# Decoding's intermediate word in PSUM, low-half products in a row, and other slots for the second batch's keys and values and the last weight's halves

## The chip, the cores and the metric

The kernel runs on one core of a Trainium2 chip, as one launch. The metric is device microseconds of that core, lower is better. The core has five engines that run their own instructions in order and wait for each other through semaphores: TensorE (PE, matmuls out of SBUF into PSUM; its weight loads are PEld), VectorE (DVE), ScalarE (ACT), GpSimd (POOL), and SyncE (SP), which issues all the DMA transfers here. SBUF and PSUM have 128 partitions; PSUM has eight banks of 512 float32 per partition, all in use.

## The reference

Three stages; q, k and v are float32, the weights float64:

```python
scores = scale * q @ k.T                      # 4 batches, 8 heads, 576 x 576, head size 64
kth = 32nd largest of each row
attn = softmax(where(scores >= kth, scores, -1e9))
x = (attn @ v) as [2304, 512]
h = x @ w_in;  x = (h * sigmoid(h)) @ w_out   # 512 -> 2048 -> 512
h = x @ w2_in; x = elu(h) @ w2_out            # 512 -> 2048 -> 512
```

The four weight matrices have 512 x 2048 elements each and arrive as float64, 8.4 MB a matrix.

## The kernel before

**Slots.** The work is a hand-ordered software pipeline, `slot(s)` for s from about -5 to 176. The 2304 rows are 18 chunks of 128, and each chunk has 8 heads, which makes 144 attention tiles: slot s holds tile s. In its slot and the next a tile gets its 32nd largest score by four MAX8 (L561) with three replacements between them (L565), and a mask with the row sum (L589), all on VectorE; ScalarE takes the exponential (L576) and the half-precision copy (L615), POOL the remainder of that copy (L621, L622), SyncE transposes both (L624), and TensorE multiplies by the values (L643) three slots later. The product of queries and keys for tile s+1 (L529) goes to TensorE in slot s, into one of two score tiles. VectorE's list of each slot is interleaved by `dv`: one operation of the top-32, then up to `per` steps of decoding.

The two MLPs follow in steps of a quarter chunk, the first from slot 13 on (`LAG`), the second from slot 25: TensorE makes h (L699), ScalarE and POOL make the activation (L727 and a subtraction L164), and two slots later TensorE multiplies by the second weight into bank `a` (L747).

**Decoding.** A weight is 16 pieces of 128 x 512 float64. A transfer (L249) brings a piece's words into a staging place (parts of W that are empty yet, for the last weight also tiles of the MLP). ScalarE or POOL shifts the low word (L259, L261). VectorE takes the high word: L271 masks and shifts it, L274 merges in the sign and exponent bit, in the same place f of W; POOL adds the low word (L277), which gives float32. The pieces lie in slots -2 to 12 by the table `PIECES` (3, 3, 4, six times 5, six times 4), 16 a weight; ten pieces of the last weight come as two halves (256 wide). Loads of the third weight stand in the slots in which the same places have just been decoded, some in the slot that decodes them.

**Scale and low halves.** When a weight is decoded, TensorE sums its Gram matrix (`w_gram`, 64 matmuls, L291, bank `a`), VectorE takes the trace a slot later (`w_trace`, L296), TensorE adds it over the partitions (L173), and a power-of-two scale follows. For the first three weights ScalarE then writes the high half (L308), TensorE forms the scaled remainder in PSUM (`w_lo`, L314 and L315) and ScalarE copies it out as the low half (L319). This goes by pairs of pieces at three points of a slot (`w_point`), in the three slots behind each weight's end, 3, 3 and 2 pairs. The last weight is scaled on ScalarE and split on POOL instead (`w_split`, L333 and L164), one or two pieces a slot.

**Second batch's keys and values.** They are loaded, squared and summed, scaled, split and stored to DRAM ahead of use (`k_keep`, `v_keep`), a key pair every four slots from slot 17 on and a value pair two slots behind each; they come back by transposing (L405) or plain loads when the chunk begins that needs them, from slot 31 on.

PSUM holds two score tiles of two banks, two rotating banks `h` (both for the MLP's h and for the low halves), one bank `a` and one for the attention output.

Of the kernel before, what the change touches and what calls it, by code (L numbers as in the profile page):

```python
# [32 lines left out]
def kernel(  # L33
# [52 lines left out]
    dram = pool("dram", 1, space=bass.MemoryType.DRAM)  # L86
    p2_p = pool("p2", 6)
    ps_s = pool("ps_s", 2, space=PSUM)
    ps_h = pool("ps_h", 2, space=PSUM)
    ps_a = pool("ps_a", 1, space=PSUM)  # L90
    ps_v = pool("ps_v", 1, space=PSUM)

# [170 lines left out]
    def w_dec_ops(j, n, e=None):  # L263
        f = w_raw(j, n, Wi)
        if e is not None:
            f = f[:, e * 256:(e + 1) * 256]
        def word(x):
            return raws[j, n, e].rearrange("p (x two) -> p x two", two=2)[:, :, x]

        def first():  # L270
            nc.vector.tensor_scalar(f, word(1), 0x07FFFFFF, 3, op0=ALU.bitwise_and, op1=ALU.logical_shift_left)  # L271

        def second():
            nc.vector.scalar_tensor_tensor(  # L274
                f, word(1), -(1 << 30), f, op0=ALU.bitwise_and, op1=ALU.bitwise_or
            )
            nc.gpsimd.tensor_tensor(f, f, word(0), op=ALU.add)  # L277

        return [first, second]
# [30 lines left out]
    los = {}  # L310

    def w_lo(j, n):
        ps = ps_h.tile([128, 512], F32, tag="h", name="lo")
        nc.tensor.matmul(out=ps, lhsT=eye[:, 128 * j:128 * j + 128], rhs=w_raw(j, n), start=True, stop=False)  # L314
        nc.tensor.matmul(out=ps, lhsT=minus, rhs=W[:, j * NWP + n, 0:DM], start=False, stop=True)  # L315
        los[j, n] = ps
# [368 lines left out]
    def emit_in(l, ch, i):  # L685
        if (l, i) == (0, 0):

            t = small.tile([128, 1], F32, tag="c1", name="c1")
            nc.gpsimd.tensor_scalar(t, ixs[:, xc(ch):xc(ch) + 1], sW[0][1], 0.5, op0=ALU.mult, op1=ALU.mult)
            c1[ch] = t  # L690
        xt = xts[l, ch]
        ps = ps_h.tile([128, 512], F32, tag="h", name="h")
        for u in range(4):
            for kk in range(KDM):
                n = 2 * l * NWP + i * 4 + kk
                f = u * 128
                wh, wl = W[:, n, f:f + 128], W[:, n, 512 + f:512 + f + 128]
                for x, (w, z) in enumerate(((wh, kk), (wh, KDM + kk), (wl, kk))):
                    nc.tensor.matmul(  # L699
                        out=ps[:, f:f + 128],  # L700
                        lhsT=w,
                        rhs=xt[:, z, :],
                        start=(kk == 0 and x == 0),
                        stop=(kk == KDM - 1 and x == 2),
                    )
        hps[l, ch, i] = ps
# [100 lines left out]
    LDB = 28  # L807
    LAG = 13
    LAG2 = 12
    SPLIT = (3, 3, 3)  # L810
    PIECES = (3, 3, 4, 5, 5, 5, 5, 5, 5, 4, 4, 4, 4, 4, 4)
    ON_ACT = 3

# [25 lines left out]
    for (b, i), t in first_use.items():  # L839
        x = dict(b=b, i=i)  # L840
        if b == 0:
            prep((t - 5, t - 4, t - 3), partial(k_load, **x), partial(k_sum, **x), True,
                 partial(k_ops, **x), partial(k_hi, **x), partial(k_lo, **x))
            late[t - 2].append((partial(k_tp, **x), None))
            prep((t - 1, t, t + 1), partial(v_load, **x), partial(v_sum, **x), True,
                 partial(v_ops, **x), partial(v_hi, **x), partial(v_lo, **x))
        else:
            d = 2 if b == 1 else 4
            r = first[b] - 35 + 2 * d * i + (19 if b == 1 else 2 * (b % 2))
            prep((r - 1, r + 1, r + 2), partial(k_load, **x), partial(k_sum, **x), True,  # L850
                 partial(k_ops, **x), partial(k_hi, **x), partial(k_keep, **x))
            late[t - 3].append((partial(k_tp, **x), None))
            r += d
            prep((r - 1, r + 1, r + 2), partial(v_load, **x), partial(v_sum, **x), True,
                 partial(v_ops, **x), partial(v_hi, **x, keep=True), partial(v_keep, **x))
            loads[t].append(partial(v_back, **x))
# [10 lines left out]

    wload, wnow = defaultdict(list), defaultdict(list)

    points, grams, traces, hi_late = {}, defaultdict(list), defaultdict(list), defaultdict(list)  # L870

    def spread(s, counts):
        return {(n, None): s + x for n, x in enumerate(x for x, c in enumerate(counts) for _ in range(c))}
# [5 lines left out]
    for j, d in dec.items():  # L879
        end = max(d.values()) + 1  # L880
        for x, s in d.items():
            decs[s].append((j, *x))
        grams[end - 1].append(j)
        traces[end].append(j)
        if j == 3:
            for (n, _), x in spread(end, (1, 1, 1, 1, 1, 1, 1, 2, 2, 1, 1, 1, 1, 1)).items():
                late[x].append((partial(w_scaled, j, n), None))
                splits[x + 1].append(partial(w_split, j, n))
            continue
        hi_late[end].append((j, 0))  # L890
        for p in range(NWP // 2):
            points[end + 1 + p // SPLIT[j], p % SPLIT[j]] = (j, p)
    late[15].append((w_const, lambda: None))
    for n in range(NWP):
        wload[(-5, -5, -4, -4, -4, -4, -3, -3, -2, -2, -2, -1, -1, -1, -1, -1)[n]].append((0, n, None))
# [8 lines left out]
    def w_point(s, p):  # L904
        if (s, p) not in points:
            return lambda: None
        j, x = points[s, p]
        for n in (2 * x, 2 * x + 1):
            w_lo(j, n)

        def rest():
            for n in (2 * x, 2 * x + 1):
                w_put(j, n)
            if 2 * x + 2 < NWP:
                w_hi2(j, x + 1)

        return rest

# [185 lines left out]
```

## Time and profile before

| what | value |
|---|---|
| median of three runs | 1182.84 us (1180.58 to 1187.54) |
| the profiled execution | 1180.23 us, its span 1178.5 us |
| busy share of the span | PE 86%, DVE 84%, ACT 74%, POOL 71% |
| mean granted TensorE clock | 0.967 |
| L277, POOL's addition | 75 in all, 55 of them at 1418 ns on average |
| L621, L727, L164 (gh) on POOL | 1162, 1271, 1160 ns on average |

A row of the 40 slices has a digit for each fortieth of the span, the busy share in tenths. In a table of stretches each row has the stretch, its length, and then for each engine the busy time and the number of instructions that start in it; at the end stand the granted clock, the share of the DMA engines and GB/s. A row of one line has the count, then the shortest, middle and longest duration in ns. A row of the timeline has start, duration, engine, line, operation and tiles, and in brackets how long the engine had been idle and what ended that.

### The profile page before, as it was taken

How to read it: one execution, taken by the hardware profiler on the slowest of the kernel's cores; microseconds unless marked ns; L12 is line 12 of the kernel's file. 1: busy time of each engine (PE TensorE's matmuls, PEld its weight loads, DVE VectorE, ACT ScalarE, POOL GpSimd, SP SyncE). 2: the span in 40 equal slices, each digit the busy share in tenths (PEclk: the TensorE clock that was granted, in tenths of full speed). 3: DMA queues.
4: the chain of work that ended last, by engine and by line, in shares of the span. 5: the costliest groups of instructions: out<-in, count | busy, mean ns of one | idle time of the engine just before them, and what ended most of it. 6: DMA issues, size and time to landing. Idle time of an engine off the chain costs nothing.

```text
span 1178.5 us, 30959 instructions
## 1 busy us (share of the span) xinstructions
PE 1016.3 (86%) x11974; PEld 727.3 (62%) x11974; DVE 984.5 (84%) x2215; ACT 875.6 (74%) x1568; POOL 841.4 (71%) x1026
## 2 busy tenths in 40 slices
PE   0057667858889999999999999999999999999997
PEld 0033233645657777677766777677777777777765
DVE  7999999997878899998988999898989999995000
ACT  6347767668787788888877888888777877777654
POOL 6777886779777667778776777677776776666643
PEclk9967889979999999999999999999999999999999
DMA  9867674353668746555567756556773654433100
GB/s 324 248 196 197 211 186 123 78 110 90 121 129 141 150 91 130 102 115 112 108 129 144 142 95 122 98 99 132 121 135 67 107 91 83 83 61 68 28 8 21
DMA packets 387157, 141.37 MB, mean 120 GB/s; under 512 B 362945, under 2 KB 370113, under 8 KB 387009
## 3 DMA queue, kind: packets, MB, share of 16 engines
q1 hardware_dynamic: 387008, 139.39, 55.7%
q8 instruction: 94, 1.54, 0.5%
q14 instruction: 55, 0.44, 0.1%
HBM read 52.17 MB, written 21.10 MB: 62 GB/s over the span
## 4 chain that ended last, share of the span: by engine, by line
PE 32%; POOL 19%; DVE 16%; DMA 15%; issue 10%; ACT 7%; SPq 1%; POOLq 0%; ACTq 0%; DVEq 0%
PE a L747 14%; PE h L699 14%; DMA et<-e 10%; POOL e L621 5%; DVE W L274 4%; POOL t L727 4%; DVE W L271 4%; DVE m L561 3%; POOL gh L164 3%; DVE r L565 3%; PE S L529 2%; PE av L643 2%; POOL e L622 1%; DMA vd<-v 1%; DMA W<-in_moe_w_in_dram 1%
## 5 line engine op out<-in xcount | busy, mean ns | idle before, releaser
L699 PE MATMUL h<-xt,W 128*128 128x128 f16 x6912 | 411.3, 220 | 2.0 <-DMA xt<-x 2.0
L747 PE MATMUL a<-W,gh 128*128 128x512 f16 x1728 | 401.6, 382 | 12.2 <-ACT o L793 5.8
L699 PEld LDWEIGHTS <-W 128*128 128x128 f16 x6912 | 396.3, 98 | 15.0 <-issue 4.5
L561 DVE MAX8 m<-r 128x8 f32<-128x576 f32 x432 | 312.9, 750 | 2.3
L747 PEld LDWEIGHTS <-gh 128*128 128x128 f16 x1728 | 160.3, 98 | 189.4 <-issue 11.6
L621 POOL TENSOR_TENSOR e<-e,e 128x512 f16<-128x512 f32 x144 | 167.4, 1162 | 139.2 <-ACT e L615 130.8
L164 POOL TENSOR_TENSOR gh<-t,gh 128x512 f16<-128x512 f32 x144 | 167.0, 1160 | 71.0 <-ACT gh L731 71.0
L565 DVE MATCH_REPLACE8 r<-m,r 128x576 f32<-128x576 f32 x288 | 214.0, 743 | 0.0
L727 POOL TENSOR_TENSOR t<-u,t 128x512 f32<-128x512 f32 x144 | 183.0, 1271 | 29.4 <-ACT u L721 23.1
L731 ACT ACTIVATE gh<-t 128x512 f16<-128x512 f32 x144 | 90.2, 627 | 116.0 <-POOL t L727 114.8
L529 PE MATMUL S<-kt,qt 128*128 128x288 f16 (+1 forms) x640 | 99.4, 297 | 64.0 <-DVE e L589 24.9
L576 ACT ACTIVATE e<-S,bias,c 128x576 f32<-128x576 f32 x144 | 119.8, 832 | 43.8 <-DVE r L565 36.3
L561 DVE MAX8 m<-S 128x8 f32<-128x576 f32 x144 | 109.6, 761 | 50.8 <-PE S L529 50.3
L615 ACT ACTIVATE e<-e 128x576 f16<-128x576 f32 x144 | 97.4, 677 | 59.7 <-DMA et<-e 26.9
L529 PEld LDWEIGHTS <-qt 128*128 128x128 f16 (+1 forms) x640 | 56.4, 102 | 134.5 <-issue 52.1
L589 DVE SCALAR_TENSOR_TENSOR e<-S,m,e 128x576 f32<-128x576 f32 x144 | 115.4, 802 | 0.1
L565 DVE MATCH_REPLACE8 r<-m,S 128x576 f32<-128x576 f32 x144 | 107.7, 748 | 0.0
L643 PE MATMUL av<-vt,et 128*128 128x64 f16 (+1 forms) x2240 | 91.6, 195 | 17.3 <-DMA et<-e 17.2
L643 PEld LDWEIGHTS <-et 128*128 128x128 f16 (+1 forms) x2240 | 80.1, 102 | 28.7 <-DMA et<-e 21.6
L314 PE MATMUL lo<-W,eye 128*128 128x512 f32 x96 | 63.7, 751 | 31.1 <-ACT W L319 22.8
L277 POOL TENSOR_TENSOR W<-W 128x512 int32<-128x512 int32 (+1 forms) x55 | 77.0, 1418 | 17.8 <-DVE W L274 7.9
L574 ACT ACTIVATE bias<-m,fixed,c 128x1 f32<-128x1 f32 x144 | 54.0, 375 | 11.1 <-DVE m L561 11.1
(125 smaller groups left out, 1218.5 us busy)
## 6 DMA issues: line engine op xcount, KB each, us to landing
W<-in_moe_w_in_dram SPq DMA_DIRECT2D x32, 512.0 KB, 6.9
W<-in_moe_w_out_dram SPq DMA_DIRECT2D x22, 512.0 KB, 5.9
qd<-q SPq DMA_DIRECT2D x34, 256.0 KB, 4.3
kn<-in_k_dram SPq DMA_DIRECT2D x16, 288.0 KB, 3.2
qn<-in_q_dram SPq DMA_DIRECT2D x16, 256.0 KB, 3.6
out_dram<-o SPq DMA_DIRECT2D x16, 256.0 KB, 2.8
vd<-v SPq DMA_DIRECT2D x12, 320.0 KB, 3.7
vt<-vd SPq DMA_DIRECT2D x24, 160.0 KB, 2.7
```

The lines of the kernel that those rows point to most:

```text
L164: nc.gpsimd.tensor_tensor(dst, x, hi, op=ALU.subtract)
L529: nc.tensor.matmul(out=ps[n * e:n * e + n, a, 0:HALF], lhsT=qt[:, 2 * (t % 2) + p, n * e:n * e + n], rhs=kt[:, a * HALF:(a + 1) * HALF], s ...
L561: nc.vector.max(st["m8"][:, i, :], src if i == 0 else st["r"])
L565: nc.vector.match_replace(out=fold(r) if i == 0 else r, in_to_replace=st["m8"][:, i, :], in_values=src if i == 0 else r, imm_value=LOW,)
L576: nc.scalar.activation(out=fold(e), in_=src, func=AF.Exp, scale=c[:, 0:1], bias=bias)
L589: nc.vector.scalar_tensor_tensor(e, src, st["m8"][:, n - 1, 7:8], e, op0=ALU.is_ge, op1=ALU.mult, accum_out=acc)
L615: nc.scalar.activation(out=h[:, 0:S], in_=e32s[t], func=AF.Copy)
L621: nc.gpsimd.tensor_tensor(h[:, S + LO:2 * S], e[:, 0:SF], h[:, 0:SF], op=ALU.subtract)
L643: nc.tensor.matmul(out=o, lhsT=et[:, c, n * e:n * e + n], rhs=r, start=(i == 0), stop=(i == len(seq) - 1))
L699: nc.tensor.matmul(out=ps[:, f:f + 128], lhsT=w, rhs=xt[:, z, :], start=(kk == 0 and x == 0), stop=(kk == KDM - 1 and x == 2),)
L727: nc.gpsimd.tensor_tensor(t, u, t, op=ALU.add if l else ALU.mult)
L747: nc.tensor.matmul(out=acc, lhsT=gh[:, z, u * 128:(u + 1) * 128], rhs=W[:, n, w * 512:(w + 1) * 512], start=(m == 0 and x == 0), stop=(m = ...
```

## The change

Five things, all in the work before slot 40:

1. L271 writes its word into a new PSUM tile y in bank `h0`, and L274 reads it from there and writes f as before. POOL's addition is unchanged. The two banks `h` no longer rotate but have names, `h0` and `h1`; the MLP alternates them by step.
2. The low-half products use `h1` for even pieces and bank `a` for odd ones, and `h1` for both in the slots in which the Gram sum holds `a` (slots 3, 6, 9, 14).
3. Their pairs form one list over the three weights, filled from slot 4 to 13 into the points that are free: three a slot, one in slots 6 and 9. Pairs end in slot 13 instead of 12.
4. The last weight's Gram sum and trace come one slot later, its scaling begins in slot 14 instead of 13, and the two doubled slots move: 17 and 19 for the scaling instead of 20 and 21.
5. The second batch's key pairs go by 16, 21, 27, 32 (before 18, 22, 26, 30) and its value pairs by 18, 24, 30, 35 (before 20, 24, 28, 32).

```diff
-    ps_h = pool("ps_h", 2, space=PSUM)
+    ps_h = pool("ps_h", 1, space=PSUM)
...
         def first():
-            nc.vector.tensor_scalar(f, word(1), 0x07FFFFFF, 3, op0=ALU.bitwise_and, op1=ALU.logical_shift_left)
+            y.append(ps_h.tile([128, 512], F32, tag="h0", name="y").bitcast(I32)[:, 0:f.shape[1]])
+            nc.vector.tensor_scalar(y[0], word(1), 0x07FFFFFF, 3, op0=ALU.bitwise_and, op1=ALU.logical_shift_left)
 
         def second():
             nc.vector.scalar_tensor_tensor(
-                f, word(1), -(1 << 30), f, op0=ALU.bitwise_and, op1=ALU.bitwise_or
+                f, word(1), -(1 << 30), y[0], op0=ALU.bitwise_and, op1=ALU.bitwise_or
             )
...
     def w_lo(j, n):
-        ps = ps_h.tile([128, 512], F32, tag="h", name="lo")
+        ps = ps_a.tile([128, 512], F32, tag="a", name="lo") if n % 2 and slot_now[0] not in held else ps_h.tile([128, 512], F32, tag="h1", name="lo")
...
-        ps = ps_h.tile([128, 512], F32, tag="h", name="h")
+        ps = ps_h.tile([128, 512], F32, tag=f"h{i % 2}", name="h")
...
-            d = 2 if b == 1 else 4
-            r = first[b] - 35 + 2 * d * i + (19 if b == 1 else 2 * (b % 2))
+            d, r = 4, first[b] - 35 + 8 * i + 2 * (b % 2)
+            if b == 1:
+                r, d = ((16, 2), (21, 3), (27, 3), (32, 3))[i]
...
-        grams[end - 1].append(j)
-        traces[end].append(j)
+        grams[end - (j < 3)].append(j)
+        traces[end + (j == 3)].append(j)
+        held.add(end + (j == 3))
         if j == 3:
-            for (n, _), x in spread(end, (1, 1, 1, 1, 1, 1, 1, 2, 2, 1, 1, 1, 1, 1)).items():
+            for (n, _), x in spread(end + 1, (1, 1, 1, 2, 1, 2, 1, 1, 1, 1, 1, 1, 0, 1, 1)).items():
...
+    pairs = [(j, p) for j in range(3) for p in range(NWP // 2)]
+    free = [(s, p) for s in range(ends[0] + 1, LAG + 1) for p in range(3) if p == 2 or s not in held]
+    points = dict(zip(free, zip(pairs, pairs[1:] + [None])))
```

VectorE in slot 1, where the first weight's last pieces are decoded between two tiles' top-32 operations (W is the weight array, S scores, r the row without the values found, m8 the maxima). Before:

```order
L561 MAX m8_336<-S_297 128x8
L271 TENSOR_SCALAR W_135<-W_135 128x512 [waits DMAHW6_49]
L274 SCALAR_TENSOR_TENSOR W_135<-W_135 128x512 [waits DVE_49]
L565 MATCH_REPLACE r_280<-m8_279,r_280 128x576
L271 TENSOR_SCALAR W_135<-W_135 128x512 [waits DMAHW7_49]
```

and in the changed kernel:

```order
L564 MAX m8_347<-S_307 128x8
L274 TENSOR_SCALAR y_350<-W_135 128x512 [waits DMAHW6_49,DVE_49]
L277 SCALAR_TENSOR_TENSOR W_135<-W_135,y_350 128x512 [waits DVE_49]
L568 MATCH_REPLACE r_287<-m8_286,r_287 128x576
L274 TENSOR_SCALAR y_355<-W_135 128x512 [waits DMAHW7_49,DVE_49]
```

Nothing moved; the first operation writes y, the second reads it, and the first also waits for VectorE's own operation before, since y has one buffer. All later line numbers are three or more higher.

TensorE at the end of slot 5, the last low-half product of the slot and the beginning of the second weight's Gram sum. Before:

```order
L315 MATMUL lo<-W,eye 128x512 [waits Activation_49]
L291 LDWEIGHTS W
L291 MATMUL gram<-W 128x128
```

and in the changed kernel:

```order
L318 MATMUL lo<-W,eye 128x512 [waits Activation_49]
L294 LDWEIGHTS W
L294 MATMUL gram<-W 128x128 [waits Activation_49]
```

The order is the same, but the Gram sum now waits for ScalarE, which copies the odd product out of the bank. The sums of the third and fourth weight have the same wait.

POOL in slot 22 (e16 is the exponentials' remainder, t and gh the MLP, x16 the second MLP's input, W a piece of the last weight). Before:

```order
L621 TENSOR_TENSOR e16_2588<-e32_2445,e16_2588 128x512
L622 TENSOR_TENSOR e16_2588<-e32_2445,e16_2588 128x64
L727 TENSOR_TENSOR t_2567<-u_2566,t_2567 128x512
L164 TENSOR_TENSOR x16_2599<-y_2371,x16_2599 128x512
L333 TENSOR_SCALAR W_135<-W_135 128x512
L164 TENSOR_TENSOR W_135<-W_135 128x512
L333 TENSOR_SCALAR W_135<-W_135 128x512
L164 TENSOR_TENSOR W_135<-W_135 128x512
L164 TENSOR_TENSOR gh_2677<-t_2567,gh_2677 128x512
```

and in the changed kernel:

```order
L624 TENSOR_TENSOR e16_2673<-e32_2541,e16_2673 128x512
L625 TENSOR_TENSOR e16_2673<-e32_2541,e16_2673 128x64
L730 TENSOR_TENSOR t_2652<-u_2651,t_2652 128x512
L164 TENSOR_TENSOR x16_2685<-y_2462,x16_2685 128x512
L336 TENSOR_SCALAR W_135<-W_135 128x512
L164 TENSOR_TENSOR W_135<-W_135 128x512
L164 TENSOR_TENSOR gh_2759<-t_2652,gh_2759 128x512
```

One of the two pieces that were split here has moved to another slot.

## Rows read from the trace of the kernel before

**Rows 1.** The page's 40 slices, busy tenths of VectorE

```profile
DVE  7999999997878899998988999898989999995000
```

**Rows 2.** Table of stretches, all engines: busy us (instructions), clock, DMA share, GB/s

```profile
44.10:106.30 62.20, 26.84 (x153) 13.83 (x154) 60.58 (x112) 34.83 (x65) 48.41 (x47) 0.79 0.71 203
106.30:146.60 40.30, 30.66 (x171) 15.66 (x170) 36.93 (x74) 31.19 (x57) 30.96 (x30) 0.84 0.71 210
146.60:204.40 57.80, 40.36 (x206) 19.04 (x204) 56.84 (x111) 38.79 (x72) 44.77 (x58) 0.87 0.64 159
...
265.40:319.90 54.50, 44.41 (x543) 32.43 (x544) 42.95 (x112) 45.50 (x83) 47.79 (x59) 0.97 0.45 100
...
400.80:1074.00 673.20, 654.66 (x8274) 488.39 (x8273) 620.10 (x1441) 542.13 (x968) 485.05 (x619) 1.00 0.58 108
```

**Rows 3.** Table of stretches, VectorE's L271 alone (first four), then L274 alone

```profile
0.00:44.10 44.10, 14.21 (x15) 1.00 0.95 305
44.10:106.30 62.20, 16.07 (x20) 0.79 0.71 203
106.30:146.60 40.30, 7.73 (x13) 0.84 0.71 210
146.60:204.40 57.80, 16.50 (x26) 0.87 0.64 159
...
0.00:44.10 44.10, 14.65 (x15) 1.00 0.95 305
44.10:106.30 62.20, 21.55 (x20) 0.79 0.71 203
106.30:146.60 40.30, 12.63 (x12) 0.84 0.71 210
146.60:204.40 57.80, 18.32 (x25) 0.87 0.64 159
```

**Rows 4.** Single lines L271 and L274: shortest, middle, longest ns

```profile
L271 DVE TENSOR_SCALAR W<-W x55: 401/824/2352, 6.8 to 199.9; 128x512 int32<-128x512 int32 x54, 128x256 int32<-128x256 int32 x1
...
L274 DVE SCALAR_TENSOR_TENSOR W<-W x55: 665/911/1771, 7.2 to 200.5; 128x512 int32<-128x512 int32 x54, 128x256 int32<-128x256 int32 x1
...
L274 DVE SCALAR_TENSOR_TENSOR W<-gh,W x6: 424/426/597, 155.0 to 198.9; 128x256 int32<-128x256 int32 x6
```

**Rows 5.** Timeline, two POOL additions and the VectorE operations issued during them

```profile
19.53 1.34 POOL L277 TENSOR_TENSOR W<-W 128x512 int32<-128x512 int32 x1 [0.68 <-DVE W L274]
19.77 1.65 DVE L274 SCALAR_TENSOR_TENSOR W<-W 128x512 int32<-128x512 int32 x1
...
35.60 1.28 POOL L277 TENSOR_TENSOR W<-W 128x512 int32<-128x512 int32 x1 [1.14 <-DMA vn<-in_v_dram]
36.12 1.05 DVE L271 TENSOR_SCALAR W<-W 128x512 int32<-128x512 int32 x1
```

**Rows 6.** Single lines of VectorE with one operand in PSUM

```profile
L760 DVE TENSOR_SCALAR y<-a x18: 671/673/692, 242.9 to 1131.9; 128x512 f32<-128x512 f32 x18
...
L589 DVE SCALAR_TENSOR_TENSOR e<-S,m,e x144: 793/801/819, 43.3 to 1073.7; 128x576 f32<-128x576 f32 x144
```

**Rows 7.** Timeline in slot 5: the loads' issue, and POOL waiting for one

```profile
96.11 2.65 SPq L249 DMA_DIRECT2D W<-in_moe_w_in_dram  x5
...
100.42 0.88 POOL L261 TENSOR_SCALAR W<-W 128x512 int32<-128x512 uint16 x1 [3.82 <-DMA W<-in_moe_w_in_dram]
```

**Rows 8.** Timeline of TensorE, the fourth weight's Gram sum at the end of slot 12

```profile
204.95 3.83 PE L291 MATMUL gram<-W 128*128 128x128 bf16 x64
```

**Rows 9.** Costs of splitting on POOL (205 to 330 us), and VectorE's gap (timeline)

```profile
L164 POOL TENSOR_TENSOR W<-W 128x512 f16<-128x512 f32 x16 | 18.5, 1159 | 1.3
...
L333 POOL TENSOR_SCALAR W<-W 128x512 f16<-128x512 f32 x16 | 9.9, 621 | 0.6 <-ACT W L161 0.6
...
278.52 0.16 DVE L133 TENSOR_SCALAR p<-S 128x1 int32<-128x1 int32 x1 [5.71 <-PE S L173]
```

**Rows 10.** Timeline, VectorE's wait for the first keys' sum

```profile
15.06 0.16 DVE L133 TENSOR_SCALAR p<-S 128x1 int32<-128x1 int32 x1 [1.15 <-PE S L173]
```

More of the change, by code (lines that the diff above doesn't have):

```diff
@@ L268, in word @@
             return raws[j, n, e].rearrange("p (x two) -> p x two", two=2)[:, :, x]
+        y = []
         def first():
-            nc.vector.tensor_scalar(f, word(1), 0x07FFFFFF, 3, op0=ALU.bitwise_and, op1=ALU.logical_shift_left)
+            y.append(ps_h.tile([128, 512], F32, tag="h0", name="y").bitcast(I32)[:, 0:f.shape[1]])
+            nc.vector.tensor_scalar(y[0], word(1), 0x07FFFFFF, 3, op0=ALU.bitwise_and, op1=ALU.logical_shift_left)
         def second():
             nc.vector.scalar_tensor_tensor(
-                f, word(1), -(1 << 30), f, op0=ALU.bitwise_and, op1=ALU.bitwise_or
+                f, word(1), -(1 << 30), y[0], op0=ALU.bitwise_and, op1=ALU.bitwise_or
             )
@@ L809 @@
     LAG2 = 12
-    SPLIT = (3, 3, 3)
     PIECES = (3, 3, 4, 5, 5, 5, 5, 5, 5, 4, 4, 4, 4, 4, 4)
@@ L868 @@
     wload, wnow = defaultdict(list), defaultdict(list)
-    points, grams, traces, hi_late = {}, defaultdict(list), defaultdict(list), defaultdict(list)
+    ends, held, grams, traces, hi_late = [], set(), defaultdict(list), defaultdict(list), defaultdict(list)
     def spread(s, counts):
@@ L889 @@
             continue
-        hi_late[end].append((j, 0))
-        for p in range(NWP // 2):
-            points[end + 1 + p // SPLIT[j], p % SPLIT[j]] = (j, p)
+        ends.append(end)
+    pairs = [(j, p) for j in range(3) for p in range(NWP // 2)]
+    free = [(s, p) for s in range(ends[0] + 1, LAG + 1) for p in range(3) if p == 2 or s not in held]
+    points = dict(zip(free, zip(pairs, pairs[1:] + [None])))
+    hi_late[ends[0]].append(pairs[0])
     late[15].append((w_const, lambda: None))
@@ L906, in w_point @@
             return lambda: None
-        j, x = points[s, p]
+        (j, x), more = points[s, p]
         for n in (2 * x, 2 * x + 1):
@@ L913, in rest @@
                 w_put(j, n)
-            if 2 * x + 2 < NWP:
-                w_hi2(j, x + 1)
+            if more:
+                w_hi2(*more)
         return rest
```

## The prediction

> **What bounds the kernel now.** I read the table of 40 slices first [rows 1]: VectorE is nearly full from the second slice to the thirty-sixth, that is through the whole attention, so averages don't tell which engine sets the pace where. So I cut the span at the ends of VectorE's mask operation (L589), one per slot, and read the busy times of these stretches [rows 2]. Between 44.1 and 106.3 us VectorE works 60.58 of 62.20 us, and between 146.6 and 204.4 us 56.84 of 57.80: there it sets the pace, with GpSimd (POOL) at 48.41 and 44.77 us behind it. Between 106.3 and 146.6 us it has 3.4 us of gaps. From 265.4 to 319.9 us nobody is full, and from 400.8 to 1074 us TensorE is, at 654.66 of 673.20 us.
>
> The early stretch is the decoding of the float64 weights: 64 pieces, of which 10 come as halves, so 54 whole pieces and 20 halves, each with one L271, one L274 and one POOL addition L277. The rows of the two lines by stretch [rows 3] sum to 55.2 and 68.0 us, 123 us of the first 206. Their spread says more than the sums [rows 4]: the same whole L271 takes 401 ns at best, 824 in the median and 2352 at worst; L274 takes 665, 911 and 1771. The timeline shows on what the rest goes [rows 5]. POOL's L277 runs from 19.53 to 20.87; L274, issued at 19.77, ends at 21.42, 0.55 us behind it. Another L277 runs from 35.60 to 36.88; L271, issued at 36.12, ends at 37.17, 0.29 us behind it. Both wait for POOL's operation to end and then do their work. MAX8 and the replacements between them never stretch.
>
> **The intermediate word in PSUM.** L271 now writes y, a tile in bank h0, and L274 reads it from there. Two prices change. First, L271 alone becomes slower: its 401 ns for 512 elements is the fast form, and the nearest row of a VectorE scalar operation with one side in PSUM is L760, 673 ns for the same 512 [rows 6]. Ends for L271 are therefore 401 ns (nothing is lost) and 824 ns (nothing is won); I take 670, the row with the same size and one PSUM side. L274 keeps 690 (665 at best; L589, which also has one operand in PSUM and one in SBUF, takes 801 for 576 elements and at most 819 in 144 runs, with POOL busy beside it [rows 4, 6]). A half costs about 0.40 and 0.43 (424 ns is the half's L274 at best [rows 4]). Sum: 54 x (0.67 + 0.69) + 20 x (0.40 + 0.43) = 90 us instead of 123, 33 us less on VectorE.
>
> The Trainium skill speaks against the first half of this. "VectorE: DVE Perf Modes", section "Why PSUM operands drop a tier", says that an fp32 operation with a PSUM operand loses the mode that streams one tensor through both read ports. By that rule alone, with no contention to win, L271 loses 0.27 us a piece. The same skill's "SBUF — State Buffer", section "Who interferes with whom", says that VectorE's second port pair is an exclusive lock shared with GpSimd, taken by a two-port mode or two SBUF inputs; the trace agrees, with 0.29 and 0.55 us of work behind each POOL operation.
>
> The change also adds a wait: each L271 waits for the L274 before it, since y has one buffer. In most places a MAX8 or replacement stands between them, so that wait is over by then; where none does, the wait costs about the overlap that is lost, some 0.1 us, and with 74 pieces mostly separated I put it inside the 0.67.
>
> **How much of the 33 us reaches the end, stretch by stretch** (before from [rows 3], after at the prices above):
> - 0 to 44.1: 15 pieces, 28.9 against 20.4, 8.5 less. The first three pieces lie before 15.06 us, where VectorE has waited 1.15 us for the first keys' sum [rows 10]. Their six rows, the longest L271 of all among them (2352 ns [rows 4]), take 6.8 us, at the new prices 4.1: 2.7 of the saving only lengthen that wait. 5.8 remain.
> - 44.1 to 106.3: 20 pieces, 37.6 against 27.2, 10.4 less. POOL's 48.41 us [rows 2] fit into the 52 that are left, and its own additions shrink too. Some transfers arrive closer to their use: I take 9.
> - 106.3 to 146.6: 20.4 against 17.0, 3.4 less. Here another loop closes. The third weight's pieces are loaded in the slot that decodes them: SyncE issues five loads at 96.11, behind the transpose of the slot, and POOL, in its order, stands at L261 for 3.82 us until 100.42 for one of them [rows 7]; its five additions come behind, then the next slot's subtraction (L621), then the next transpose and the next loads. VectorE saves nothing there that this loop does not give back. 1.5.
> - 146.6 to 204.4: 34.8 against 24.2, 10.6 less, with loads of the same kind for the fourth weight's halves. 7.
>
> That is 23.3 us.
>
> **Low-half products in a row.** Three points a slot stay, but slots 6 and 9 keep one instead of two, because the Gram sum holds the bank that the odd products now use. The last pairs move to slot 13, and the fourth Gram sum with them, one slot later. Its 3.83 us on TensorE [rows 8] now stand in slot 13 behind the first MLP product instead of ahead of it. All Gram sums after the first now wait for ScalarE's copy out of the odd product; VectorE's trace comes half a slot later, so I cost that at nothing, and if this cover is gone, VectorE stands for one copy and a Gram sum, up to 5 us each. Two pairs of products more lie in slots 12 and 13; TensorE has 17 us idle in the 57.8 before [rows 2], so most is absorbed. From 0 to 5 us lost; I take 2.
>
> **Keys, values and the last weight's halves in other slots.** Each splitting of a piece costs POOL 0.62 + 1.16 us [rows 9]. Before, two pieces each stand in slots 21 and 22, with a key pair's subtraction in 21, the second MLP's input in 22 and a value in 23; with the mean durations of the other lines (in the table ahead) POOL has about 6.7, 8.8 and 7.1 us there, for slots of some 6. After, it has 4.9, 7.0 and 5.7, and 7.3 in slot 24. The consequence before is the longest gap of VectorE after decoding, 5.71 us up to 278.52, where TensorE's sum sits behind an output product that waits for POOL [rows 9]. I expect 4 of these 5.7 us back. The ends are 0 (the pile moves to slot 24) and 8, since TensorE's 44.41 us leave 10 idle in that stretch [rows 2]. ScalarE's and SyncE's parts of the keys and values keep their number; the last value is stored two slots before it is read back, where it was five before, which covers one landing.
>
> Total: 23.3 - 2 + 4 = 25.3 us. Behind slot 40 everything is TensorE's steady work and only shifts. The profiled execution has 1180.23 us around its span of 1178.5, 2.6 below the median of the three runs, 1182.84; against the median I get 1157.5, rounded to 1157.
>
> **Rivals.**
> 1. The loop through POOL and the loads decides in every decoding slot, not in three. For it: POOL waits for loads in its own order [rows 7]. Against it: VectorE's gaps outside 106 to 146 us are small, so the loop has slack now. Then the first stretch's 5.8 and half of the second and fourth (10.5) remain, nothing of the third; less 3 for the Gram sum: 13 us, 1170.
> 2. Everything arrives: 33 less 2.7, plus the whole 8 of the keys and halves, nothing lost on TensorE: 38 to 41 us, 1143.
> 3. The change doesn't do what it says: the stretched rows are no waiting for POOL, or writing PSUM brings a wait of its own. Then L271 only loses its fast form, 54 x 0.27 + 20 x 0.13 = 17 us, 1200. The rows that end a fixed time behind POOL speak against it. This is also what the tier rule alone would give.
> 4. Slower by TensorE's order: in slots 5, 8 and 13 the Gram sum waits for a copy that stands behind ScalarE's other work, and VectorE, in order, stands at the trace. At 5 us each this takes 15 of the 25; it decides from 9 us each, and then gives 1185 to 1193.
>
> **How the numbers follow.** The forecast, with sizes between rivals 1 and 2, has 0.60; rival 1 0.17, rival 2 0.13, rival 3 0.03, rival 4 0.03, and 0.04 for gains and losses that cancel to within half a per cent. Half a per cent, 6 us, is about what a measurement of this kernel can tell from no change. Rival 1 lies inside the range, rival 2 at its edge; 1143 to 1173 leaves out about 2 in 10. Faster by over 0.5%: 0.60 + 0.17 + 0.13 = 0.90. Same: 0.05, slower: 0.05, from rivals 3 and 4 and the rest.
>
> **What the changed profile would show.** L271's successor at 0.65 to 0.70 us with hardly any spread, L274's at 0.67 to 0.72, POOL's L277 near 1.28 always, as in the second pair of [rows 5]; VectorE's slots of five pieces at about 13 us instead of 15 to 16, those around the third weight hardly shorter, with gaps for loads; decoding over near 180 instead of 204 us; no gap of 5 us in slots 22 to 24. I'm wrong if the two operations still stretch to ends behind POOL's, if VectorE's gaps for loads grow to over 10 us in all, or if the trace waits for the Gram sum.

## The result

| kernel | median | range | ratio to the kernel before |
|---|---|---|---|
| before, beside the changed kernel | 1181.71 us (4 runs) | 1178.38 to 1187.54 | |
| changed | 1149.53 us (4 runs) | 1148.67 to 1150.49 | 0.9723 [0.9682, 0.9763] |

The changed kernel is faster by 32 us, where 25 were forecast; 1149.53 us lies inside the range, about halfway between the forecast and the 38 to 41 us of the prediction's rival 2. Its profiled execution took 1149.13 us around a span of 1147.4, against 1178.5. All later lines of the code are three or more higher: L271 is now L274, L274 is L277, POOL's addition L277 is L280.

The 40 slices of VectorE after the change (page, part 2), as in [rows 1]:

```profile
DVE  5998998999798989999998989989889999994000
```

It is about as full as before, in slices of 28.7 us instead of 29.5. So I cut the span again at the ends of the mask operation (L592), at the same tiles as in [rows 2]. The columns are those of [rows 2]; the row from 176.90 on has no counterpart there:

```profile
40.40:93.10 52.70, 25.53 (x152) 13.86 (x153) 50.26 (x112) 34.55 (x65) 41.03 (x47) 0.81 0.90 258
93.10:128.90 35.80, 27.79 (x165) 14.17 (x164) 32.69 (x74) 28.90 (x54) 26.04 (x31) 0.90 0.82 241
128.90:176.90 48.00, 34.49 (x200) 16.56 (x199) 46.55 (x110) 36.58 (x69) 40.34 (x57) 0.96 0.79 191
176.90:204.50 27.60, 27.43 (x363) 21.35 (x361) 24.86 (x60) 20.30 (x36) 16.28 (x24) 1.00 0.25 53
...
241.00:286.50 45.50, 42.58 (x540) 31.36 (x540) 42.25 (x107) 41.18 (x76) 42.26 (x51) 1.00 0.50 104
```

Set beside the stretches of before, by the tile whose mask ends them:

| stretch | before, us | after, us | gain | forecast |
|---|---|---|---|---|
| to mask 0 | 44.1 | 40.4 | 3.7 | 5.8 |
| masks 0 to 4 | 62.2 | 52.7 | 9.5 | 9 |
| masks 4 to 7 | 40.3 | 35.8 | 4.5 | 1.5 |
| masks 7 to 11 | 57.8 | 48.0 | 9.8 | 7 |
| masks 11 to 21 | 61.0 | 64.1 | -3.1 | -2 |
| masks 21 to 28 | 54.5 | 45.5 | 9.0 | 4 |
| behind mask 28 | 858.6 | 860.9 | -2.3 | 0 |

The last row can't be called an effect of the change: a second profiled execution of the changed kernel had 865.4 us there, so two executions of one kernel differ by more.

The two operations of decoding and POOL's addition, as single lines (shortest, middle, longest ns), which answer [rows 4]:

```profile
L274 DVE TENSOR_SCALAR y<-W x55: 407/682/709, 8.3 to 173.8; 128x512 int32<-128x512 int32 x54, 128x256 int32<-128x256 int32 x1
...
L277 DVE SCALAR_TENSOR_TENSOR W<-W,y x55: 420/686/690, 9.0 to 174.3; 128x512 int32<-128x512 int32 x54, 128x256 int32<-128x256 int32 x1
...
L280 POOL TENSOR_TENSOR W<-W x55: 742/1288/1308, 11.1 to 175.2; 128x512 int32<-128x512 int32 x54, 128x256 int32<-128x256 int32 x1
```

The spread is gone. The longest L274 takes 709 ns where the longest L271 took 2352, and the longest L277 takes 690 where the longest L274 took 1771. The timeline shows the same next to POOL's additions, in answer to [rows 5] (start, duration; the x4 is four additions in a row):

```profile
26.32 5.04 POOL L280 TENSOR_TENSOR W<-W 128x512 int32<-128x512 int32 x4
...
26.80 0.69 DVE L274 TENSOR_SCALAR y<-W 128x512 int32<-128x512 int32 x1
...
28.13 0.68 DVE L277 SCALAR_TENSOR_TENSOR W<-W,y 128x512 int32<-128x512 int32 x1
```

Both were issued while POOL added without a break until 31.36, and both ended in 0.7 us.

VectorE's waits until the end of decoding (total us, times, longest):

```profile
DVE p L133 <- PE S L173: 7.5, 2, 3.8
DVE y L274 <- DMA W<-in_moe_w_in_dram: 5.1, 3, 2.2
```

And between masks 21 and 28, where [rows 9] had 5.71 us at once:

```profile
DVE m L564 <- PE S L532: 1.4, 2, 1.0
DVE sum L1015 <- POOL sum L148: 1.0, 1, 1.0
DVE p L133 <- PE S L173: 0.8, 1, 0.8
```

Loads keep VectorE waiting 5.1 us in all, where it was 4.8 before, and the gap of 5.71 us has shrunk to 1.0. What has grown is the wait for the keys' sums in the first stretch, 7.5 us.

### The profile page after: what moved, and what is told of

Read it like the earlier page. It is cut to its first block, busy times and chain, and to the rows that moved or that the text cites. A ratio compares the mean times of both kernels' runs of the same rounds, so it can differ in the third digit from the quotient of the medians.

```text
span 1147.4 us, 31015 instructions
## 1 busy us (share of the span) xinstructions
PE 1011.7 (88%) x11974; PEld 723.8 (63%) x11974; DVE 952.2 (83%) x2215; ACT 874.8 (76%) x1568; POOL 820.7 (72%) x1026
## 4 chain that ended last, share of the span: by engine, by line
PE 29%; POOL 23%; DMA 12%; issue 11%; ACT 7%; SPq 2%; DVE 1%; POOLq 0%; ACTq 0%
PE h L702 13%; PE a L750 12%; DMA et<-e 8%; POOL e L624 7%; POOL t L730 6%; POOL gh L164 4%; PE S L532 2%; PE av L646 2%; POOL e L625 2%; ACT gh L734 1%; POOL x L164 1%; DMA qt<-qd 1%; POOL v L164 1%; DMA vd<-v 1%; ACT e L618 1%
## 5 line engine op out<-in xcount | busy, mean ns | idle before, releaser
L702 PEld LDWEIGHTS <-W 128*128 128x128 f16 x6912 | 395.6, 98 | 13.2 <-issue 2.8
L592 DVE SCALAR_TENSOR_TENSOR e<-S,m,e 128x576 f32<-128x576 f32 x144 | 115.3, 800 | 0.1
L317 PE MATMUL lo<-W,eye 128*128 128x512 f32 x96 | 58.5, 694 | 20.0 <-ACT W L322 19.1
L280 POOL TENSOR_TENSOR W<-W 128x512 int32<-128x512 int32 (+1 forms) x55 | 69.0, 1278 | 9.3 <-DVE W L277 3.5
L724 ACT ACTIVATE u<-u,c 128x512 f32<-128x512 f32 x72 | 58.6, 814 | 2.4
```

The source lines that it names most:

```text
L592: nc.vector.scalar_tensor_tensor(e, src, st["m8"][:, n - 1, 7:8], e, op0=ALU.is_ge, op1=ALU.mult, accum_out=acc)
L702: nc.tensor.matmul(out=ps[:, f:f + 128], lhsT=w, rhs=xt[:, z, :], start=(kk == 0 and x == 0), stop=(kk == KDM - 1 and x == 2),)
```

## The experiments

### What makes the two operations stretch

My theory was that VectorE's two operations and POOL's share one way into SBUF, and that y in PSUM takes VectorE out of it. One rival: the stretching comes from reading and writing the same place (f), so that any other place for y would do. So y goes to a tile of its own in SBUF for the first three weights, and nothing else changes against the kernel before:

```diff
-            nc.vector.tensor_scalar(f, word(1), 0x07FFFFFF, 3, op0=ALU.bitwise_and, op1=ALU.logical_shift_left)
+            y.append(f if j == 3 else xt_p.tile([128, 2 * KDM, 128], F16, tag="xt0", name="y").rearrange("p a x -> p (a x)").bitcast(I32))
+            nc.vector.tensor_scalar(y[0], word(1), 0x07FFFFFF, 3, op0=ALU.bitwise_and, op1=ALU.logical_shift_left)
...
-                f, word(1), -(1 << 30), f, op0=ALU.bitwise_and, op1=ALU.bitwise_or
+                f, word(1), -(1 << 30), y[0], op0=ALU.bitwise_and, op1=ALU.bitwise_or
```

> The kernel before, where for the first three weights the intermediate word goes to a tile of its own in SBUF instead of PSUM. Theory (the wait is for a way into SBUF that VectorE shares with POOL): L271's successor still takes 0.40 at best and about 0.8 in the middle, L274's 0.67 at best and about 0.9 to 1.0; no gain, ratio 0.995 to 1.005. Rival (the wait comes from reading and writing the same place, or from a bank of W that POOL adds in): middle durations fall to 0.41 and 0.69, and the three weights gain 20 us or more, ratio under 0.983.

Measured: 1185.23 us, ratio 1.0013 [0.9997, 1.0028]. The single lines of this kernel:

```profile
L274 DVE TENSOR_SCALAR y<-W x48: 400/830/1405, 6.3 to 146.5; 128x512 int32<-128x512 int32 x48
...
L277 DVE SCALAR_TENSOR_TENSOR W<-W,y x48: 666/954/2655, 6.8 to 148.0; 128x512 int32<-128x512 int32 x48
```

The operations stretch as before, up to 2655 ns, and all of them together take 123 us, as before. Another place in SBUF doesn't help; a place in PSUM does.

The other half of the theory is POOL. In this kernel, otherwise that of before, POOL's addition of the low word is left out (the weights are then only the high words):

```diff
-            nc.gpsimd.tensor_tensor(f, f, word(0), op=ALU.add)
```

> The kernel before without POOL's addition of the low word (that part of the decoding is left out, so the weights lack it). Theory (POOL's own operations are what the two operations wait for): with 74 of POOL's two-input additions gone, L271 takes 0.40 and L274 0.67 to 0.69 in the middle, with a few stretched beside the other POOL operations; VectorE's sum for both falls from 123 to 75 to 85 us; mask 11 ends between 165 and 178 us. Rival (they wait for transfers or for ScalarE's writes into the same rows): middle durations stay above 0.8 and 0.9, and mask 11 stays above 195 us.

Measured in one run: 1155.25 us; mask 11 at 174.0 us, where it was 204.4 before and is 176.9 after the change. The single lines:

```profile
L271 DVE TENSOR_SCALAR W<-W x55: 275/418/2186, 8.1 to 171.2; 128x512 int32<-128x512 int32 x54, 128x256 int32<-128x256 int32 x1
...
L274 DVE SCALAR_TENSOR_TENSOR W<-W x55: 424/693/1534, 8.6 to 171.5; 128x512 int32<-128x512 int32 x54, 128x256 int32<-128x256 int32 x1
```

The middle L271 falls from 824 to 418 ns and the middle L274 from 911 to 693, near their shortest of 401 and 665 [rows 4]. So POOL's addition is most of what holds VectorE up. The longest are still 2186 and 1534 ns, since POOL's other operations stay: the longest L271 ends at 11.54 us, 0.28 behind POOL's subtraction for the queries, and the longest L274 at 143.17, 0.55 behind POOL's remainder of the exponentials. These are about the distances of [rows 5], 0.29 and 0.55, behind operations other than the addition. The sum of both lines is 91 us, where I had expected at most 85. Taking all of POOL's additions away thus gives hardly more than the PSUM word, which keeps them.

### The PSUM word alone, and why the products go in a row

Here the kernel before gets y in bank h0 and the odd products in bank `a`, with the three points of a slot, the Gram sums and the other slots as before. In the slots that hold `a` for the Gram sum both products of a pair use h1:

```diff
-        ps = ps_h.tile([128, 512], F32, tag="h", name="lo")
+        ps = ps_a.tile([128, 512], F32, tag="a", name="lo") if n % 2 and slot_now[0] not in (3, 6, 9, 13) else ps_h.tile([128, 512], F32, tag="h1", name="lo")
```

> The kernel before with part 1 of the change alone: the word in PSUM, and the banks that it needs (odd low-half products in bank a, none of them moved to other slots; Gram sums, keys, values and halves as before). Theory (the gain of the decoding is VectorE no longer waiting for POOL): mask 11 ends at about 177 us, as in the changed kernel, instead of 204; the stretch behind it costs nothing extra since the fourth Gram sum stays in slot 12; the whole is 27 us faster than before, ratio 0.977 (0.973 to 0.981). Rival (the gain needs the products in a row, since TensorE or ScalarE would hold the decoding up): mask 11 not before 187 us, ratio 0.985 or more.

Measured: 1166.79 us, ratio 0.9855 [0.9833, 0.9876]. I had expected 0.977; over a third of the gain is missing, and the ratio is where my rival put it (0.985 or more), while mask 11, at 185.4 us, ends between the theory's 177 and the rival's 187. The two operations take 0.68 us as in the changed kernel, and masks 0 to 4 take 52.7 us as there. But masks 4 to 7 take 39.9 us instead of 35.8 and masks 7 to 11 52.5 instead of 48.0. VectorE's waits between 93 and 186 us say why:

```profile
DVE p L133 <- PE gram L173: 8.8, 2, 5.0
```

The timeline of this kernel from the end of slot 5 through slot 6 shows the longer of the two:

```profile
102.12 3.83 PE L294 MATMUL gram<-W 128*128 128x128 bf16 x64 [2.19 <-ACT W L322]
...
112.07 1.13 PE L317 MATMUL lo<-W,eye 128*128 128x512 f32 x2 [0.94 <-ACT W L322]
...
113.25 0.17 PE L173 MATMUL gram<-wm,fixed 128*128 128x1 bf16 x1
...
113.48 0.16 DVE L133 TENSOR_SCALAR p<-gram 128x1 int32<-128x1 int32 x1 [5.01 <-PE gram L173]
```

The Gram sum starts 2.19 us late, behind ScalarE's copy out of `a`. Behind it stand two pairs with one bank, each product waiting for the copy of the one before, and only then TensorE's sum over the partitions, for which VectorE stands 5.01 us. That is the price of the prediction's rival 4, at 5.0 us in slot 6 and 3.8 in slot 9, and in part its mechanism: rival 4 has the Gram sum late behind a copy, but the pairs behind the sum are what VectorE stands for. In the changed kernel the Gram sums wait as long for a copy (3.6 us in two places, in both kernels), and VectorE's wait is gone, since its list takes two pairs out of slots 6 and 9: masks 0 to 11 differ by 8.6 us between the two kernels.

### The keys, the values and the halves

The new slots alone, on the kernel before:

```diff
-            d = 2 if b == 1 else 4
-            r = first[b] - 35 + 2 * d * i + (19 if b == 1 else 2 * (b % 2))
+            d, r = 4, first[b] - 35 + 8 * i + 2 * (b % 2)
+            if b == 1:
+                r, d = ((16, 2), (21, 3), (27, 3), (32, 3))[i]
...
-            for (n, _), x in spread(end, (1, 1, 1, 1, 1, 1, 1, 2, 2, 1, 1, 1, 1, 1)).items():
+            for (n, _), x in spread(end + 1, (1, 1, 1, 2, 1, 2, 1, 1, 1, 1, 1, 1, 0, 1, 1)).items():
```

> The kernel before with the other slots for the second batch's keys and values and for the last weight's halves alone; the decoding is as before. Theory (POOL's pile in slots 21 to 23 is spread, whatever the decoding does): nothing changes before mask 11, the stretch from mask 21 to mask 28 takes 45 to 47 us instead of 54.5, ratio 0.992 to 0.994. Rival (the 9 us there come from the faster decoding, which shifts loads and ScalarE's work): ratio 0.997 to 1.002 and the stretch stays over 52 us.

Measured: 1174.51 us, ratio 0.993 [0.9907, 0.9954]; masks 21 to 28 take 45.6 us, as expected. And the changed kernel with the old slots for both:

> The changed kernel with the old slots for the keys and values, and the halves doubled in the same slots 20 and 21 as before. Theory: the decoding as in the changed kernel (mask 11 at 177 us), the pile of POOL is back: mask 21 to 28 in 52 to 56 us, the whole 1156 to 1160, ratio 0.980. Rival (the decoding gives the 9 us): 1150, ratio 0.973.

Measured: 1159.38 us, ratio 0.9794 [0.9769, 0.9818]; masks 21 to 28 take 54.6 us. Its edit is the last diff read backwards, but the list of the halves keeps its new start and has one entry less ahead of the doubled slots, so that these stay 20 and 21. The stretch after mask 21 thus depends on the slots alone, and the rest of the change on the other parts: 0.993 x 0.9794 is 0.9725, beside the changed kernel's 0.9723.

Which of the two slots it is was tried by putting back one at a time, in the changed kernel. First the old slots of keys and values:

> The changed kernel with the old slots for the second batch's keys and values; the halves keep their new slots. With the halves alone moved, POOL has one split fewer in slots 21 and 22, but a key pair's subtraction in 21 and a value in 23 again. Theory (the doubled halves made the pile): mask 21 to 28 in 46 to 49 us, the whole 1150 to 1153. Rival (the keys and values made it): 53 to 55 us, 1157 to 1160.

Measured: 1156.78 us, ratio 0.9773 [0.974, 0.9806]; masks 21 to 28 take 54.4 us. All nine microseconds are gone, though the pile of halves had moved. My theory fell here, and the rival's 53 to 55 us held. Then the old doubled slots of the halves:

```diff
-            for (n, _), x in spread(end + 1, (1, 1, 1, 2, 1, 2, 1, 1, 1, 1, 1, 1, 0, 1, 1)).items():
+            for (n, _), x in spread(end + 1, (1, 1, 1, 1, 1, 1, 2, 2, 1, 1, 1, 1, 1, 1)).items():
```

> The changed kernel with the last weight's halves doubled in slots 20 and 21 again; keys and values keep their new slots. Theory (the doubled halves made the pile): mask 21 to 28 in 52 to 54 us, the whole 1156 to 1159. Rival (the keys and values made it): 45 to 47 us, 1149 to 1151.

Measured: 1154.56 us, ratio 0.9744 [0.9715, 0.9773]; masks 21 to 28 take 49.7 us, 4.2 more than in the changed kernel and between the theory's 52 to 54 and the rival's 45 to 47. The ratios of these two runs overlap with that of the changed kernel; what separates them is this stretch, in one profiled execution each. The stretch comes out alike where the slots are alike: 45.5 and 45.6 us with both new, 54.5 and 54.6 with both old. The timeline of the kernel with the old halves shows the pile that I had predicted, engine by engine:

```profile
244.09 0.62 POOL L336 TENSOR_SCALAR W<-W 128x512 f16<-128x512 f32 x1
244.79 1.16 POOL L164 TENSOR_TENSOR W<-W 128x512 f16<-128x512 f32 x1
...
245.92 0.62 POOL L336 TENSOR_SCALAR W<-W 128x512 f16<-128x512 f32 x1
...
246.62 1.15 POOL L164 TENSOR_TENSOR W<-W 128x512 f16<-128x512 f32 x1
...
247.74 1.15 POOL L164 TENSOR_TENSOR gh<-t,gh 128x512 f16<-128x512 f32 x1
...
248.95 4.45 PE L750 MATMUL a<-W,gh 128*128 128x512 f16 x10 [2.82 <-POOL gh L164]
...
253.19 1.04 PE L532 MATMUL S<-kt,qt 128*128 128x288 f16 x4
...
254.27 0.77 DVE L564 MAX8 m<-S 128x8 f32<-128x576 f32 x1 [6.46 <-PE S L532]
```

POOL splits two pieces, the activation (gh) comes behind them, TensorE waits 2.82 us for it with the next scores behind, and VectorE waits 6.46 us for these.

With keys and values in the old slots another wait stands out. The longest of TensorE's waits between masks 21 and 28 in that kernel:

```profile
PE av L646 <- DMA et<-e: 11.0, 5, 4.0
```

It waits for the exponentials' transposes, 11.0 us in all. The same wait has 5.6 us in the kernel before and 0.7 in the changed one. So there are two causes, one in each slot table, that lie beside each other: alone, the halves' new slots bring nothing (54.4 against 54.6 us), those of keys and values 4.9 (49.7), both 9.1 (45.5). The trace of the kernel with the old key slots shows how the longest of these waits arises:

```profile
265.57 2.61 SPq L369 DMA_DIRECT2D qn<-in_q_dram  x4
...
268.29 1.36 SPq L627 DMA_TRANSPOSE et<-e  x1
```

The loads of queries (qn) and of key pairs (kn) share two buffers. With the old slots a key pair is loaded just ahead of the queries (259.94 us), and SyncE, in order, stands 5.6 us at L369. It goes on at 265.57, when POOL's subtraction for a key pair has ended (265.55) and its buffer is free. The transpose, whose input POOL had ready at 262.93, is issued only behind these loads, and TensorE waits 4.04 us for it until 271.62. The kernel before has the same 5.6 us of SyncE and 3.3 of TensorE behind it; the kernels with the new key slots show no wait at that line. What this one wait is worth was not tried, and the other transposes' waits stay open.

### Three tries behind the change

In masks 4 to 7 VectorE still waits 1.4 us for the third weight's loads, which SyncE issues behind a transpose (and 1.3 us for scores). Here the changed kernel issues them first, in all slots:

```diff
+        for x in wload[s - 1]:
+            w_load(*x)
         if LDA <= s < LDB:
...
-        for x in wload[s - 1]:
-            w_load(*x)
```

> The changed kernel with the weights' loads of a slot issued ahead of that slot's transpose of the exponentials instead of behind it; nothing else moves. Theory (with VectorE faster, the loop of POOL's additions, transpose and loads is next in masks 4 to 7): the gap of 1.4 us before the decoding operation in masks 4 to 7 goes, and POOL waits less at its word operation; 1 to 3 us faster than the changed kernel, 1147 to 1149. Rival (the loads wait for their places to come free, not for the transpose): nothing, 1149 to 1151, or a loss, since the transposes now come later.

Measured: 1150.28 us, ratio 0.9703 [0.9673, 0.9734]. Masks 4 to 7 take 32.9 us instead of 35.8, masks 7 to 11 49.9 instead of 48.0, and the wait for the keys' sums in the first stretch is 10.3 instead of 7.5 us. The waits for loads went, as the theory said, and the time stayed where the rival put it. The next three ran side by side, with the changed kernel among them:

> The changed kernel as it stands, beside the next two in one comparison: ratio to the kernel before between 0.968 and 0.977, some 1150 us, as when it was first timed. It is the base of the next two.

Measured: 1153.0 us (1148.61 to 1155.71), ratio 0.9726 [0.97, 0.9752]; mask 28 at 286.5 us, as in its first profile. Then the loads ahead in slots 5 to 8 alone (`if 5 <= s <= 8:` around the moved lines, `if not 5 <= s <= 8:` where they were):

> The changed kernel with the weights' loads ahead of the transposes in slots 5 to 8 alone. Theory (the loop of POOL, transpose and loads costs about 3 us around the third weight, and the 2 us lost between masks 7 and 11 came from the loads put ahead there, where the transposes wait behind them): masks 4 to 7 about 33 us, masks 7 to 11 about 48, span 2 to 4 us under that of the changed kernel. Rival (VectorE's saving there is given back later whatever the loads do, since POOL has the same work in all): masks 7 to 11 again near 50, span as that of the changed kernel.

Measured: 1150.89 us, ratio 0.9721 [0.9698, 0.9744]. Masks 4 to 7 take 32.9 us, but masks 7 to 11 now 52.4: 3.4 us won against the run beside it, 4.4 given back. The rival's outcome held, though POOL's work, its reason, is not what shows. The timeline of this kernel behind mask 7, which ends at 124.0 us, shows into what the saving turns:

```profile
125.96 1.23 ACT L259 ACTIVATE W<-W 128x512 int32<-128x512 uint16 x2
...
127.50 0.83 ACT L579 ACTIVATE e<-S,bias,c 128x576 f32<-128x576 f32 x1
128.22 1.08 ACT L322 ACTIVATE W<-lo 128x512 f16<-128x512 f32 x2
...
128.87 1.12 PE L317 MATMUL lo<-W,eye 128*128 128x512 f32 x2 [1.48 <-ACT W L322]
...
131.25 0.65 PE L532 MATMUL S<-kt,qt 128*128 128x288 f16 x4
...
131.94 0.77 DVE L564 MAX8 m<-S 128x8 f32<-128x576 f32 x1 [4.20 <-PE S L532]
```

ScalarE has shifts of decoding and an exponential ahead of its copies out of the low-half products, TensorE waits for these copies with the next scores behind, and VectorE, now early, waits 4.20 us for the scores. Last, the same with four of the first weight's six loads moved behind the second key load:

```diff
-        wload[(-5, -5, -4, -4, -4, -4, -3, -3, -2, -2, -2, -1, -1, -1, -1, -1)[n]].append((0, n, None))
+        wload[(-5, -5, -3, -3, -3, -3, -3, -3, -2, -2, -2, -1, -1, -1, -1, -1)[n]].append((0, n, None))
```

> The same, and the second key load ahead of four of the first weight's loads that stood before it. Theory (the first stretch gave 3.7 us where 5.8 were forecast because VectorE waits for the keys' sums, 7.5 us in the changed kernel, and those wait for a load behind six loads of 512 KB): the wait at L133 falls from 7.5 to below 4 us, mask 0 ends 2 to 4 us earlier, at 37 to 39 us, and the span is 4 to 7 us under that of the changed kernel. Rival (the first pieces then come later, and decoding waits instead): mask 0 at 40 to 41 us, waits of VectorE for the first weight's loads grow by what the keys' sums give.

Measured: 1148.72 us (1145.23 to 1154.13), ratio 0.9701 [0.9674, 0.9729]. VectorE's waits until 180 us:

```profile
DVE m L564 <- PE S L532: 5.8, 2, 3.4
DVE p L133 <- PE S L173: 3.8, 1, 3.8
DVE y L274 <- DMA W<-in_moe_w_in_dram: 2.6, 3, 1.4
```

The wait for the keys' sums is halved, as expected, but in the first stretch 2.4 us of waiting for the first scores and a little more for loads (2.6 us there, where it was 2.3) stand in its place, and mask 0 ends at 39.6 us instead of 40.5. That is neither the theory's 37 to 39 nor the rival's 40 to 41. The interval overlaps that of the changed kernel, so none of the three is shown to be better than it.

## Why the prediction was right

**The price of the word in PSUM.** Forecast 0.67 and 0.69 us for whole pieces, 0.40 and 0.43 for halves; measured 0.68 and 0.68, 0.42 and 0.42. The sum is 90.5 us, forecast 90. The row of the same size with one side in PSUM, L760 in [rows 6], gave the price, and [rows 5] the cause; the two runs on y in SBUF and without the addition show it. The wait for y's one buffer is no part of these durations: where nothing stands between, L274 starts 0.73 us behind the L277 before it (8.99 and 9.72 us), where a MAX8, which need not wait, starts 0.60 behind an L274 (20.80 and 21.40). That is about the 0.1 us a place that the prediction took.

The Trainium skill, "VectorE: DVE Perf Modes", section "Why PSUM operands drop a tier", had said that the PSUM operand costs the fast form; the trace agrees, with 0.68 us where 0.40 was the best before, and the loss, 17 us by the prediction's rival 3, is outweighed by the waiting that goes, since the sum still falls from 123 to 90.5 us.

**The first stretch, 5.8 forecast, 3.7 measured.** The step that failed is a term that I left out: I held the time of the keys' sum [rows 10] and of the loads fixed. The pieces became 8.3 us shorter, against 8.5 forecast, and the wait for the keys' sums grew from 5.0 to 7.5 us in two places, 2.5 where I had 2.7. But VectorE also waits 2.2 us for loads where it had waited 1.0, and the second of the two sums came 1.31 us later than the 15.06 of before:

```profile
16.37 0.16 DVE L133 TENSOR_SCALAR p<-S 128x1 int32<-128x1 int32 x1 [3.79 <-PE S L173]
```

The load of its keys was issued at 5.76 us instead of 4.88, because SyncE took 4.02 us instead of 3.13 to issue the six loads ahead of it. This need not come from the change: with the slots alone, where decoding is that of before, the sum came at 16.25 us and mask 0 ended at 45.3; in the changed kernel with the old slots it came at 15.50, and mask 0 ended at 39.5. Where the sums come at nearly the same time, the first stretch thus gains 4.9 us (45.3 against 40.4) and 4.6 (44.1 against 39.5). The 0.9 to 1.2 us that are still missing I have not traced.

**Masks 0 to 4, 9 forecast, 9.5 measured**, in slots of 13.2 us as the prediction said they would be.

**Masks 4 to 7, 1.5 forecast, 4.5 measured; masks 7 to 11, 7 forecast, 9.8 measured.** Here the step was wrong: "VectorE saves nothing there that this loop does not give back". The loop through POOL, the transposes and the loads [rows 7] exists, and POOL still waits 5.4 us for loads in it, at most 5.0 at once. But I held its length fixed, and the stretch that it paces became 4.5 us shorter. POOL's groups in masks 4 to 7 before (count, busy us and mean ns, idle time ahead of them):

```profile
L277 POOL TENSOR_TENSOR W<-W 128x512 int32<-128x512 int32 x11 | 15.9, 1472 | 0.2
L261 POOL TENSOR_SCALAR W<-W 128x512 int32<-128x512 uint16 x7 | 5.5, 780 | 6.9 <-DMA W<-in_moe_w_in_dram 4.8 <-DVE m L561 1.7
...
L622 POOL TENSOR_TENSOR e<-e,e 128x64 f16<-128x64 f32 x3 | 2.2, 748 | 0.0
```

and after:

```profile
L280 POOL TENSOR_TENSOR W<-W 128x512 int32<-128x512 int32 x12 | 15.2, 1288 | 0.2
L261 POOL TENSOR_SCALAR W<-W 128x512 int32<-128x512 uint16 x7 | 4.7, 672 | 5.8 <-DMA W<-in_moe_w_in_dram 5.4
...
L625 POOL TENSOR_TENSOR e<-e,e 128x64 f16<-128x64 f32 x3 | 0.9, 308 | 0.0
```

POOL's operations had been stretched by VectorE as well: 748 ns against 308 for the smallest. The timeline of before shows the same a little earlier, between masks 3 and 4:

```profile
92.83 1.68 DVE L274 SCALAR_TENSOR_TENSOR W<-W 128x512 int32<-128x512 int32 x1
...
93.92 0.75 POOL L622 TENSOR_TENSOR e<-e,e 128x64 f16<-128x64 f32 x1
```

POOL's subtraction ends at 94.67 us, 0.16 behind L274's end at 94.51. All three of masks 4 to 7 end 0.17 us behind an L274 (110.61 behind 110.44, 129.01 behind 128.84, 143.58 behind 143.41). POOL's busy time in this stretch fell from 30.96 to 26.04 us, 4.9 us. The waiting was mutual, and I priced one side of it, though the addition's 1418 ns in the table ahead against 1.28 us in [rows 5] showed the other. That POOL's shorter operations are what shortened this loop fits these numbers, but no run tries it alone. In masks 7 to 11 VectorE has no wait at all after the change, so of the 10.2 us that its two operations lost there 9.8 reach the end; my 7 was a deduction for loads that came in time.

The Trainium skill's "SBUF — State Buffer", section "Who interferes with whom", says of the port pair that whoever issues first holds it for the whole instruction and the other is blocked. The trace agrees, with POOL's 748 against 308 ns; read for both engines, that sentence would have pointed at this term.

**Low-half products in a row, -2 forecast, -3.1 measured.** The range of 0 to 5 us held, and the place too. TensorE from 183 us on, in the changed kernel:

```profile
183.30 1.08 PE L317 MATMUL lo<-W,eye 128*128 128x512 f32 x2
...
186.47 3.83 PE L294 MATMUL gram<-W 128*128 128x128 bf16 x64
190.15 2.84 PE L702 MATMUL h<-xt,W 128*128 128x128 f16 x48
```

The last pairs, the Gram sum (the 3.83 us of [rows 8]) and the MLP stand there without a gap: TensorE works 27.43 of 27.60 us between masks 11 and 15, which took 24.7 before. VectorE's waits for the fourth trace and its sum over the partitions are small there, 0.3 and 1.3 us. I was right to cost such waits at nothing, but the half slot ahead of the trace, my reason, is not enough: the run with the PSUM word alone has it too, and VectorE stood 8.8 us at the sums behind the traces. The changed kernel with the old slots waits only 1.0 us at a trace before mask 11 and never at the sums, so it is the list, which takes two pairs out of slots 6 and 9, that keeps the waits small.

**Keys, values and halves, 4 forecast, 9.0 measured.** The end of 8 was too low, and the attribution half wrong. I put all of it down to POOL's pile of halves in slots 21 and 22. That pile is real and costs 4.2 us by the run that puts it back. But the keys' and values' slots bring 4.9 us alone and 8.9 beside the halves' new ones, and the halves' slots alone 0.2: the shares depend on the order. I had costed the keys and values at nothing because their work keeps its number. Their waits lie in the trace of before: TensorE waited 5.6 us for the exponentials' transposes there, a row that I did not price.

**The total.** The missed terms have both signs: -2.1, +0.5, +3.0, +2.8, -1.1 and +5.0, which with -2.3 behind mask 28 makes the spans' 31.1 where 25.3 was forecast. The direction rested on the first term alone and held; that the total came within 6 us owes something to errors that cancel.

## What to carry to other kernels

Where one operation of an engine shows a wide spread and another of the same kind none, look for the operation of another engine whose end they share, and then price both engines without the waiting, since here each of them lost by the other. A word that is written once and read once by the same engine can go to PSUM although its fast form is lost there: here a known 0.68 us beat 0.40 that was 0.82 in the middle and 2.35 at worst. Before a bank is given to it, look which sums then stand behind the remaining bank's copies, and move these in the same change.

## What the runs showed that was not expected

- An operation of VectorE with one source in SBUF and one in PSUM (L277) never took over 690 ns in 55, with POOL adding beside it; with both sources in SBUF it took up to 1771, and up to 2655 with y in a place of its own.
- VectorE stretches POOL as well: in masks 4 to 7 a subtraction of 64 columns took 748 ns on average (three of them) where it took 308 after the change, an addition 1472 where it took 1288.
- Without POOL's addition, and with y in SBUF, the longest of VectorE's two operations still end 0.28 and 0.55 us behind an operation of POOL, now a subtraction: about the distances of [rows 5].
